# A finer split of a 512-point transform, quartered weight loads on three queues, and a priority table, in a spectral filter plus GEGLU kernel

## The chip, the cores and the metric

One core of one Trainium2 chip. The metric is device microseconds for one execution. TensorE (PE) multiplies, with its weight loads shown as PEld; VectorE (DVE), ScalarE (ACT) and GpSimd (POOL) do the rest; SyncE (SP) mostly issues DMAs, which ACT and POOL can issue too. Each engine works through its own queue in order and waits on semaphores for the others.

## The reference

The output is the sum of the input, a frequency-domain filter of its normalized rows, and a GEGLU layer of the same normalized rows:

```python
xn = _layernorm(x, axis=-1)                 # x: 1 x 2048 x 512, bf16
X  = rfft2(xn) * (w_r + 1j * w_i)           # over 2048 and 512; w: 2048 x 257
A  = irfft2(X)
h  = gelu(xn @ w_gate) * (xn @ w_up)        # 512 x 1792 each
out = x + A + h @ w_down                    # 1792 x 512
```

## The kernel before, in words

**The work.** The 2048 rows are 16 tiles of 128 rows (index j), in four blocks of four tiles (index m). For each tile DVE takes statistics (L617, L623, L631), POOL or ACT and DVE the reciprocal root (L626, L632, L633), and DVE or ACT writes the normalized row `xn` in one instruction (`ln_norm`, L641 to L647). PE transposes `xn` (`trans`, L657) and DVE or ACT copies the result to `xnT` (L668, L669): 512 features in four chunks of 128 partitions, 512 rows in the free dimension. Both branches read `xnT`.

**GEGLU.** `gate_up` (L917) makes one slice `fc` of 128 hidden features for one block: four matmuls with the gate weights (one for each chunk of features), four with the up weights (L930), a gelu on ACT (L934) and a product on DVE (L940, or L937 and L938). There are 14 slices. Block 0 does its first four slices in two halves, tiles 0 and 1 and then tiles 2 and 3, so that it can begin before the whole block is there. Blocks 2 and 3 use seven products in place of eight (`gate_up7`, L1011); the down projection does so in all blocks (L1105, and L1120 at the very end).

**Spectral branch.** The 512-point transform of a block is `butter` and `unit_D`. `butter` (L679) adds and subtracts the two halves of the features (L683, L684: 1024 elements each) and then adds and subtracts the halves of the sum (L685, L686: 512 each). `unit_D` (L688) multiplies each tile with constants `fd`: 128 columns for L697, 128 for L698, and 256 columns each for L699 and L700, which accumulate the part of the odd frequencies from the difference that was not split further. ACT writes the result to `xs` (L703). `unit_A` (L717, L720) takes the next step, its result goes through DRAM (`scr`, `tv`), and the products with the filter (L805, L826) and the way back (L855, L877) follow from about 74 us on.

**What sets the order.** Every instruction, DMAs included, is a task of a planner (`_Plan`, L215) with an engine, an estimated cost and a priority `prio`. The planner plays the tasks through in its own estimate of time: whenever an engine is free it takes, of the tasks that are ready, the one with the lowest priority number, with a bonus for a PE task of the same mode as the one before. The result is a fixed order for each engine's queue. Priorities come from a dictionary of constants, `K`, and from the arguments of the calls. A task with a `gate` also waits until the main products have come to that number.

**Loads at the start.** `load_w` (L570) loads a range of slices of one weight as one DMA: eight DMAs, all on SP, for slices 0 to 4, 4 to 8, 8 to 11 and 11 to 14 of gate and up. Tiles 0 and 1 of `x` come in halves of 64 partitions on SP and ACT, all later tiles on SP. Seventeen dummy matmuls (`warm`, L1203) run ahead of and between the first transposes.

Of the kernel before, what the change touches and what calls it, by code (L numbers as in the profile page):

```python
# [7 lines left out]
ACT = mybir.ActivationFunctionType  # L8
# [6 lines left out]
D = 512  # L15
# [14 lines left out]
def _constants():  # L30
# [9 lines left out]
    m64 = np.arange(64)[None, :]  # L40
    a0 = tp * (p + 0.5) * (4 * m64) / D
    a2 = tp * (p + 0.5) * (4 * m64 + 2) / D
    im0 = -np.sin(a0)
# [77 lines left out]
    for i, (a, b) in enumerate(((c, s), (-s, c), (-c, -s))):  # L121
# [8 lines left out]
            f16(CM), f16(G.reshape(P, -1)), f16(NA))  # L130

# [83 lines left out]
class _Plan:  # L215
# [37 lines left out]
    def schedule(self):  # L253
# [26 lines left out]
        def refill():  # L280
# [4 lines left out]
            t.i, t.eng, t.fn, t.r, t.w, t.over = len(T), "pe", (lambda e: self.fill(e, b)), (("wg", 0, 0), ("wg", 0, 1)), (("bank", b),), ()  # L285
# [136 lines left out]
def bass_parallel_sum__spectral_gfnet__glu_gated_geglu__prompt_kernel(  # L422
# [25 lines left out]
    with ExitStack() as es:  # L448
# [19 lines left out]
        tmp = area[:, 0:1024].rearrange("p (a c) -> p a c", a=2)  # L468
# [3 lines left out]
        AREA = [("tmp",)] + [("fold", i, k) for i in range(2) for k in range(3)] + [("xs", i) for i in range(4)]  # L472
# [94 lines left out]
        def wkey(nm, fs, dcs=(0, 1)):  # L567
# [13 lines left out]
        add("pool", lambda e: e.memset(nn, 0.0), w=[("nz",)], occ=1.0, lat=1.2, prio=-99)  # L581
# [22 lines left out]
        load_w("g", 11, 14, "sp", -88)  # L604
        load_w("u", 11, 14, "sp", -87)
# [35 lines left out]
        def ln_norm(j, prio, eng="dve"):  # L641
            if eng == "act":
                act(lambda e: e.activation(xn[:, j % 4, :], x_sb[:, j, :], ACT.Identity, bias=nmr[:, j:j + 1], scale=rstd[:, j:j + 1]), 770,
                    [("x", j, 0), ("x", j, 1), ("nmr", j), ("rstd", j)], [("xn", j % 4)], prio)
                return
            add("dve", lambda e: e.tensor_scalar(xn[:, j % 4, :], x_sb[:, j, :], ag[:, j, 0:1], rstd[:, j:j + 1], ALU.subtract, ALU.mult),
                r=[("x", j, 0), ("x", j, 1), ("ag", j), ("rstd", j)], w=[("xn", j % 4)], occ=0.33, lat=0.47, prio=prio)  # L647

        def trans(m, dcs, jjs, prio, eng="dve"):
# [9 lines left out]
            pe(f, [P] * (len(dcs) * len(jjs)), [("ident",)] + [("xn", jj) for jj in jjs], [("ps", v), ("tr", m, dcs, jjs)], prio, alloc=(v, 1, False))  # L659
# [19 lines left out]
        def butter(m, prio):  # L679
            f = fold[m % 2]  # L680
            k = ("fold", m % 2)
            x = xnT[m]
            dve(lambda e: e.tensor_tensor(tmp, x[:, 0:2, :], x[:, 2:4, :], ALU.add), 1024, xk(m), [("tmp",)], prio, x=2)  # L683
            dve(lambda e: e.tensor_tensor(f[:, 2:4, :], x[:, 0:2, :], x[:, 2:4, :], ALU.subtract), 1024, xk(m), [k + (1,)], prio, x=2)  # L684
            dve(lambda e: e.tensor_tensor(f[:, 0, :], tmp[:, 0], tmp[:, 1], ALU.add), 512, [("tmp",)], [k + (0,)], prio, x=2)  # L685
            dve(lambda e: e.tensor_tensor(f[:, 1, :], tmp[:, 0], tmp[:, 1], ALU.subtract), 512, [("tmp",)], [k + (2,)], prio, x=2)  # L686

        def unit_D(j, prio):  # L688
# [6 lines left out]
            def fn(e):  # L695
                o = bank(v).rearrange("p (a r c) -> p a r c", a=2, r=4)
                e.matmul(o[:, :, 0, :], f[:, 0, c], fd[:, 0:128], start=True, stop=False, skip_group_check=True)  # L697
                e.matmul(o[:, :, 2, :], f[:, 1, c], fd[:, 128:256], start=False, stop=False, skip_group_check=True)  # L698
                e.matmul(o[:, :, 1::2, :], f[:, 2, c], fd[:, 256:512], start=False, stop=False, skip_group_check=True)  # L699
                return e.matmul(o[:, :, 1::2, :], f[:, 3, c], fd[:, 512:768], start=False, stop=True, skip_group_check=True)  # L700
            pe(fn, [P, P, 256, 256], [("fd",)] + [k + (i,) for i in range(3)], [("ps", v)], prio, alloc=(v, 1, False), full=True)
# [212 lines left out]

        gun = [0]

        def gate_up(m, fc, jjs, prio, soft=()):  # L917
            k = gun[0] % 3
            gun[0] += 1
            n = len(jjs) * P  # L920
# [457 lines left out]
```

## Time and profile before

| What | Value |
|---|---|
| Runs | median 178.47 us (178.37 to 178.93, 3 runs) |
| Profiled execution | 177.96 us, of which the span is 175.80 us |
| Granted TensorE clock, mean | 0.999 |
| Busy in the span | PE 169.7, DVE 151.5, ACT 115.9, POOL 60.1 us |
| First gate product | starts at 7.46 us |
| Last matmul group | starts at 170.73 us |

The span is what the profile covers; 2.16 us of the profiled execution lie outside it. In the profile's rows, the time of an instruction runs from its start to its end; instructions of one engine overlap, since the next one starts before the last has drained. What an instruction costs its engine is therefore the distance between two starts (its pitch), which is shorter than its duration. "Idle before" names what ended a wait.

### The profile page before, as it was taken

How to read it: one execution, taken by the hardware profiler on the slowest of the kernel's cores; microseconds unless marked ns; L12 is line 12 of the kernel's file. 1: busy time of each engine (PE TensorE's matmuls, PEld its weight loads, DVE VectorE, ACT ScalarE, POOL GpSimd, SP SyncE). 2: the span in 40 equal slices, each digit the busy share in tenths (PEclk: the TensorE clock that was granted, in tenths of full speed). 3: DMA queues.
4: the chain of work that ended last, by engine and by line, in shares of the span. 5: the costliest groups of instructions: out<-in, count | busy, mean ns of one | idle time of the engine just before them, and what ended most of it. 6: DMA issues, size and time to landing. Idle time of an engine off the chain costs nothing.

```text
span 175.8 us, 4162 instructions
## 1 busy us (share of the span) xinstructions
PE 169.7 (97%) x1580; PEld 124.0 (71%) x1580; DVE 151.5 (86%) x346; ACT 115.9 (66%) x193; POOL 60.1 (34%) x104
## 2 busy tenths in 40 slices
PE   7989999999999999999999999999999999999992
PEld 2557555557758854444787788887889998888881
DVE  2689799979798755699699899998999999999992
ACT  3625997779973223388853899889928699996200
POOL 2020205458816368888678100004145120000000
PEclk9999999999999999999999999999999999999999
DMA  3999996898867877575898942400022223100013
GB/s 77 308 319 309 267 266 182 242 296 223 192 134 111 165 202 194 146 228 151 205 258 234 237 124 60 123 0 0 6 60 56 69 60 84 39 0 4 0 30 90
DMA packets 20819, 25.26 MB, mean 144 GB/s; under 512 B 3232, under 2 KB 16928, under 8 KB 20544
## 3 DMA queue, kind: packets, MB, share of 16 engines
q1 hardware_dynamic: 17088, 17.21, 36.4%
q0 software_dynamic: 3120, 7.47, 18.2%
q10 hardware_dynamic: 592, 0.33, 0.7%
q8 instruction: 12, 0.20, 0.5%
q14 instruction: 7, 0.06, 0.1%
HBM read 18.70 MB, written 6.29 MB: 142 GB/s over the span
## 4 chain that ended last, share of the span: by engine, by line
PE 83%; DVE 9%; DMA 3%; SPq 2%; issue 1%; DVEq 0%
PE ps L930 25%; PE ps L1105 23%; PE ps L1011 20%; DMA x_sb<-in_A_x_dram 3%; PE ps L826 3%; PE ps L877 2%; PE ps L657 2%; PE ps L855 2%; SPq L560 2%; PE ps L805 1%; DVE hT L1038 1%; DVE hT L1042 1%; PE ps L699 1%; PE ps L700 1%; PE ps L717 1%
## 5 line engine op out<-in xcount | busy, mean ns | idle before, releaser
L930 PE MATMUL ps<-xw,wu 128*128 128x512 f16 (+1 forms) x128 | 29.3, 353 | 0.5 <-DMA wu<-in_B_w_up_dram 0.5
L930 PE MATMUL ps<-xw,wg 128*128 128x512 f16 (+1 forms) x128 | 29.0, 353 | 0.2 <-DVE xw L668 0.2
L934 ACT ACTIVATE gl<-ps 128x512 bf16<-128x512 f32 (+1 forms) x32 | 17.3, 546 | 17.7 <-PE ps L930 17.6
L862 POOL COPY bc<-tv 1x128 bf16<-1x128 bf16 x16 | 8.7, 558 | 39.6 <-ACT bc L861 39.6
L940 DVE TENSOR_TENSOR hT<-ps,gl 128x512 bf16<-128x512 f32 (+1 forms) x26 | 15.4, 602 | 6.5 <-PE ps L930 5.6
L930 PEld LDWEIGHTS ps<-xw,wu 128*128 128x128 bf16 x128 | 12.0, 98 | 11.3 <-DMA wu<-in_B_w_up_dram 0.7
L930 PEld LDWEIGHTS ps<-xw,wg 128*128 128x128 bf16 x128 | 11.9, 98 | 10.6 <-DMA wg<-in_B_w_gate_dram 0.6
L613 POOL DMA_DIRECT2D xw<-in_A_w_r_dram x28 | 16.2, 612 | 7.9 <-PE ps L930 5.0
L1024 ACT ACTIVATE gl<-ps 128x512 bf16<-128x512 f32 x28 | 17.1, 632 | 2.1 <-PE ps L1011 1.2
L613 POOL DMA_DIRECT2D xw<-in_A_w_i_dram x28 | 16.1, 601 | 3.7 <-PE ps L1105 2.5
L1011 PE MATMUL ps<-xn,ws 128*128 128x256 f16 x112 | 16.2, 273 | 0.0
L1011 PE MATMUL ps<-xn,wu 128*128 128x256 f16 x112 | 16.0, 273 | 0.0
L1011 PE MATMUL ps<-xw,wg 128*128 128x256 f16 x112 | 16.0, 273 | 0.0
L1105 PE MATMUL ps<-wd,hT 128*128 128x256 bf16 x112 | 13.6, 273 | 0.0
L617 DVE BATCH_NORM_STATS2 st<-x_sb 128x6 f32<-128x512 bf16 x16 | 10.5, 683 | 3.5 <-DMA x_sb<-in_A_x_dram 3.3
L1105 PE MATMUL ps<-wd,hs 128*128 128x256 f16 (+1 forms) x112 | 13.4, 273 | 0.0
L1105 PE MATMUL ps<-wdt,hs 128*128 128x256 f16 x112 | 13.1, 273 | 0.0
L626 POOL TENSOR_TENSOR rstd<-vpe,mhalf 128x4 f32<-128x4 f32 (+1 forms) x5 | 4.6, 923 | 23.0 <-DVE vpe L624 23.0
L1105 PEld LDWEIGHTS ps<-wd,hT 128*128 128x128 bf16 x112 | 10.6, 98 | 2.1 <-ACT bc L861 0.3
L1105 PEld LDWEIGHTS ps<-wdt,hs 128*128 128x128 f16 x112 | 10.8, 98 | 1.6 <-issue 0.2
L1105 PEld LDWEIGHTS ps<-wd,hs 128*128 128x128 f16 x112 | 10.8, 98 | 1.6 <-DVE mu L1140 0.2
L1011 PEld LDWEIGHTS ps<-xw,wg 128*128 128x128 bf16 x112 | 10.7, 98 | 1.6 <-issue 0.2
(132 smaller groups left out, 381.9 us busy)
## 6 DMA issues: line engine op xcount, KB each, us to landing
scr<-ta SPq DMA_DIRECT2D x32, 64.0 KB, 4.9
tv<-scr SPq DMA_DIRECT2D x8, 256.0 KB, 5.6
scr<-bc SPq DMA_DIRECT2D x16, 128.0 KB, 3.1
area<-scr SPq DMA_DIRECT2D x8, 256.0 KB, 4.2
xw<-in_A_w_r_dram POOLq DMA_DIRECT2D x28, 64.0 KB, 3.8
xw<-in_A_w_i_dram POOLq DMA_DIRECT2D x28, 64.0 KB, 3.6
x_sb<-in_A_x_dram SPq DMA_DIRECT2D x6, 256.0 KB, 10.4
out_dram<-x_sb SPq DMA_DIRECT2D x12, 128.0 KB, 2.3
```

The source lines that it names most:

```text
L560: return add(eng, lambda e: e.dma_start(dst, src), r=r, w=w, over=over, occ=occ, lat=kb / 1024 / rate, prio=prio, dma=True)
L613: add("pool", lambda e: e.dma_start(dst, src), r=r, w=w, over=over, occ=0.7, lat=kb / 1024 / 0.27, prio=prio, gate=prio, dma=True)
L617: add("dve", lambda e: e.bn_stats(st[:, j, :], x_sb[:, j, :]), r=[("x", j, 0), ("x", j, 1)] + behind, w=[("st", j)], occ=0.6, lat=0.75, pr ...
L626: add("pool", lambda e: e.tensor_tensor(rstd[:, sl], vpe[:, sl], mhalf[:, 0:n], ALU.pow), r=[("vpe", j) for j in js] + [("mhalf",)], w=[(" ...
L826: ins = e.matmul(bank(v, hh)[64 * kl:64 * kl + 64, 256 * z:256 * z + 256], cm[64 * hh:64 * hh + 64, 2 * H + z, kl, i, :], pp[i][64 * hh:64 ...
L862: add("pool", lambda e: e.tensor_copy(z[0:1, 1, :].rearrange("o (b q) -> o b q", b=2), z256[0:1, :].rearrange("o (b j q) -> o b j q", b=2, ...
L930: ins = e.matmul(bank(v)[:, 0:n], w_sb[nm][:, dc, fc * P:(fc + 1) * P], xnT[m][:, dc, c0:c0 + n], start=(dc == 0), stop=(dc == 3))
L934: act(lambda e: e.activation(gl[k][:, 0:n], bank(vs[0])[:, 0:n], ACT.Gelu_apprx_tanh), n, [("ps", v)], [("gl", k)], prio)
L940: dve(lambda e: e.tensor_tensor(o, bank(vs[1])[:, 0:n], gl[k][:, 0:n], ALU.mult), n, [("ps", vs[1]), ("gl", k)], ks, prio + K["dH"])
L1011: ins = e.matmul(bank(v)[:, 256 * q:256 * q + 256], W_, B0[:, dc, :], start=(first and q == 0 and dc == 0), stop=(dc == 1), skip_group_che ...
L1024: act(lambda e: e.activation(gl[k][:], bank(v), ACT.Gelu_apprx_tanh), 512, [("ps", v)], [("gl", k)], prio + K["aG"])
L1105: ins = e.matmul(bank(v)[:, 256 * t:256 * t + 256], A0[:, f, P * t:P * t + P], B0[:, f, :], start=(first and t == 0 and f == 0), stop=(f = ...
```

## The change

It has five parts.

1. **The 512-point transform is split once more.** `ln_norm` now writes the features of a row in another order, in two instructions: in chunks 0 and 2 the two groups of 64 change places, in chunks 1 and 3 each group of 64 is reversed. With it `butter` splits the difference as well as the sum (four instructions of 512 elements in place of two), and `unit_D` becomes four matmuls of 128 columns each. `fd` shrinks from 768 to 512 columns. `tmp` becomes two buffers. The constants follow the new order.
2. **Weights.** Since the features have a new order, the rows of the gate and up weights are loaded in it: four DMAs for each range (two halves of 64 partitions for chunks 0 and 2, and one each for chunks 1 and 3). The ranges become 0 to 2, 2 to 4, 4 to 9 and 9 to 14, so 32 DMAs in place of 8. For slices 0 to 4, chunks 1 and 3 are issued by POOL; one DMA of the up weights goes to ACT, and so does one half of tiles 2 and 3 of `x`.
3. **First gate products.** For slices 0 and 1 of block 0 the gate product of two tiles is made tile by tile (128 columns at a time, eight matmuls in place of four).
4. The two dummy matmuls behind the second transpose go.
5. **Order.** A table `ORDER` gives the priority of every one of the 1072 tasks, and `GATES` the gates; they replace what `K` and the arguments set. The bonus for the same PE mode becomes 1.0 (it was 12.67).

The diff, cut to its core; the other hunks rename keys or adapt constants to the new order.

```diff
+    r = np.arange(P)[:, None] ^ 64
+    ae, ao = tp * (r + 0.5) * 2 * m / D, tp * (r + 0.5) * (2 * m + 1) / D
+    im0 = -np.sin(ae)
     im0[:, 0] = (-1.0) ** np.arange(P)
-    fo = []
-    for c in range(2):
-        kodd = np.concatenate([4 * m64[0] + 1, 4 * m64[0] + 3])[None, :]
-        a = tp * (p + P * c + 0.5) * kodd / D
-        fo += [np.cos(a), -np.sin(a)]
-    FD = np.concatenate([np.cos(a0), im0, np.cos(a2), -np.sin(a2)] + fo, 1)
+    FD = np.concatenate([np.cos(ae), im0, np.cos(ao), -np.sin(ao)], 1)
...
+ORDER = [
+    -578, 187, -235, -1622, -2527, -3409, -3271, -3914, -3516, -3004, -2669, -3101, -2614, -2693, -2697, -167, -2069, -1900, -2211, -842, -1854, -1431, -725, -541,
...
+]
+GATES = {281: 6146, 282: 5379, 283: 4832, 300: 2591, 301: 3138,
...
-        tmp = area[:, 0:1024].rearrange("p (a c) -> p a c", a=2)
+        tmp = [area[:, 1024 * i:1024 * i + 1024].rearrange("p (a c) -> p a c", a=2) for i in range(2)]
...
-        def load_w(nm, lo, hi, eng, prio, dcs=(0, 1)):
-
-            src = (B_w_gate if nm == "g" else B_w_up).rearrange("(dc p) f -> p dc f", p=P)
+        def load_w(nm, lo, hi, eng, prio, odd=None, second=None):
+
+
+            src = (B_w_gate if nm == "g" else B_w_up).rearrange("(dc i p) f -> i p dc f", i=2, p=P)
             cs = slice(P * lo, P * hi)
-            ds = slice(2 * dcs[0], 2 * dcs[-1] + 2)
-            dma(eng, w_sb[nm][:, ds, cs], src[:, ds, cs], w=wkey(nm, range(lo, hi), dcs), prio=prio, kb=64 * len(dcs) * (hi - lo))
+            n = hi - lo
+            for a in range(2):
+                dma((eng, second or eng)[a], w_sb[nm][64 * a:64 * a + 64, ::2, cs], src[0][64 - 64 * a:128 - 64 * a, :, cs], w=[(k, f, a) for k, f, _ in wkey(nm, range(lo, hi), (0,))],
+                    prio=prio + 0.01 * a + (4 if second and a else 0), kb=32 * n)
+            for i in range(2):
+                v = src[1][:, i, cs].rearrange("(a q) f -> a q f", a=2)[:, ::-1]
+                dma(odd or eng, w_sb[nm][:, 2 * i + 1, cs], v, w=[(k, f, 2 + i) for k, f, _ in wkey(nm, range(lo, hi), (0,))], prio=prio + 0.02 + 0.01 * i, kb=32 * n)
...
         dma("sp", ident[:], c_id.ap(), w=[("ident",)], prio=-99.2, kb=32)
-        load_w("g", 0, 4, "sp", -99)
+        load_w("g", 0, 2, "sp", -99, "pool")
         load_x(2, 2, 0, "sp", -98.5)
-        load_x(2, 2, 1, "sp", -98)
-        load_w("u", 0, 4, "sp", -97)
-        load_w("g", 4, 8, "sp", -96)
-        load_w("u", 4, 8, "sp", -95)
+        load_x(2, 2, 1, "act", -98)
+        load_w("u", 0, 2, "sp", -97.5, "pool")
+        load_w("g", 2, 4, "sp", -97, "pool")
+        load_w("u", 2, 4, "sp", -96.5, "pool", "act")
+        load_w("g", 4, 9, "sp", -96)
+        load_w("u", 4, 9, "sp", -95)
         amv = c_am.ap().rearrange("p (j r c) -> p j r c", j=NJ, r=2)
 
         def load_am(m, prio, eng="sp"):
             dma(eng, am[:, 4 * m:4 * m + 4], amv[:, 4 * m:4 * m + 4], w=[("am", m)], prio=prio, kb=256)
         load_x(4, 4, 0, "sp", -94.5)
         load_x(4, 4, 1, "sp", -94)
-        dma("sp", fd[:], c_fd.ap(), w=[("fd",)], prio=-93, kb=192)
+        dma("sp", fd[:, 0:512], c_fd.ap(), w=[("fd",)], prio=-93, kb=128)
         load_am(0, -92.5)
-        load_w("g", 8, 11, "sp", -92)
-        load_w("u", 8, 11, "sp", -91)
+        load_w("g", 9, 14, "sp", -92)
+        load_w("u", 9, 14, "sp", -91)
...
         def ln_norm(j, prio, eng="dve"):
-            if eng == "act":
-                act(lambda e: e.activation(xn[:, j % 4, :], x_sb[:, j, :], ACT.Identity, bias=nmr[:, j:j + 1], scale=rstd[:, j:j + 1]), 770,
-                    [("x", j, 0), ("x", j, 1), ("nmr", j), ("rstd", j)], [("xn", j % 4)], prio)
-                return
-            add("dve", lambda e: e.tensor_scalar(xn[:, j % 4, :], x_sb[:, j, :], ag[:, j, 0:1], rstd[:, j:j + 1], ALU.subtract, ALU.mult),
-                r=[("x", j, 0), ("x", j, 1), ("ag", j), ("rstd", j)], w=[("xn", j % 4)], occ=0.33, lat=0.47, prio=prio)
+
+            xq = x_sb[:, j, :].rearrange("p (d i a c) -> p i d a c", i=2, a=2, c=64)
+            o = xn[:, j % 4, :].rearrange("p (d i a c) -> p i d a c", i=2, a=2, c=64)
+            for i, (xi, oi) in enumerate(((xq[:, 0], o[:, 0][:, :, ::-1]), (xq[:, 1], o[:, 1][:, :, :, ::-1]))):
+                if eng == "act":
+                    act(lambda e, xi=xi, oi=oi: e.activation(oi, xi, ACT.Identity, bias=nmr[:, j:j + 1], scale=rstd[:, j:j + 1]), 500,
+                        [("x", j, 0), ("x", j, 1), ("nmr", j), ("rstd", j)], [("xn", j % 4, i)], prio)
+                else:
+                    add("dve", lambda e, xi=xi, oi=oi: e.tensor_scalar(oi, xi, ag[:, j, 0:1], rstd[:, j:j + 1], ALU.subtract, ALU.mult),
+                        r=[("x", j, 0), ("x", j, 1), ("ag", j), ("rstd", j)], w=[("xn", j % 4, i)], occ=0.2, lat=0.33, prio=prio)
...
-            dve(lambda e: e.tensor_tensor(tmp, x[:, 0:2, :], x[:, 2:4, :], ALU.add), 1024, xk(m), [("tmp",)], prio, x=2)
-            dve(lambda e: e.tensor_tensor(f[:, 2:4, :], x[:, 0:2, :], x[:, 2:4, :], ALU.subtract), 1024, xk(m), [k + (1,)], prio, x=2)
-            dve(lambda e: e.tensor_tensor(f[:, 0, :], tmp[:, 0], tmp[:, 1], ALU.add), 512, [("tmp",)], [k + (0,)], prio, x=2)
-            dve(lambda e: e.tensor_tensor(f[:, 1, :], tmp[:, 0], tmp[:, 1], ALU.subtract), 512, [("tmp",)], [k + (2,)], prio, x=2)
+            t, d = tmp[0], tmp[1]
+            dve(lambda e: e.tensor_tensor(t, x[:, 0:2, :], x[:, 2:4, :], ALU.add), 1024, xk(m), [("tmp", 0)], prio, x=2)
+            dve(lambda e: e.tensor_tensor(d, x[:, 0:2, :], x[:, 2:4, :], ALU.subtract), 1024, xk(m), [("tmp", 1)], prio, x=2)
+            for i, (s, op) in enumerate(((t, ALU.add), (t, ALU.subtract), (d, ALU.subtract), (d, ALU.add))):
+                dve(lambda e, i=i, s=s, op=op: e.tensor_tensor(f[:, i, :], s[:, 0], s[:, 1], op), 512, [("tmp", i // 2)], [k + (i,)], prio, x=2)
...
-                o = bank(v).rearrange("p (a r c) -> p a r c", a=2, r=4)
-                e.matmul(o[:, :, 0, :], f[:, 0, c], fd[:, 0:128], start=True, stop=False, skip_group_check=True)
-                e.matmul(o[:, :, 2, :], f[:, 1, c], fd[:, 128:256], start=False, stop=False, skip_group_check=True)
-                e.matmul(o[:, :, 1::2, :], f[:, 2, c], fd[:, 256:512], start=False, stop=False, skip_group_check=True)
-                return e.matmul(o[:, :, 1::2, :], f[:, 3, c], fd[:, 512:768], start=False, stop=True, skip_group_check=True)
-            pe(fn, [P, P, 256, 256], [("fd",)] + [k + (i,) for i in range(3)], [("ps", v)], prio, alloc=(v, 1, False), full=True)
+                ins = None
+                for i in range(4):
+                    ins = e.matmul(bank(v)[:, P * i:P * i + P], f[:, i, c], fd[:, P * i:P * i + P], start=(i == 0), stop=(i == 3), skip_group_check=True)
+                return ins
+            pe(fn, [P] * 4, [("fd",)] + [k + (i,) for i in range(4)], [("ps", v)], prio, alloc=(v, 1, False), full=True)
...
+                np_ = parts if nm == "g" else 1
+                w = n // np_
+                for i in range(np_):
+                    def fn(e, nm=nm, v=v, i=i, w=w):
+                        ins = None
+                        for dc in range(4):
+                            ins = e.matmul(bank(v)[:, w * i:w * i + w], w_sb[nm][:, dc, fc * P:(fc + 1) * P], xnT[m][:, dc, c0 + w * i:c0 + w * i + w],
+                                           start=(dc == 0 and i == 0), stop=(dc == 3), skip_group_check=True)
+                        return ins
+                    js = jjs[len(jjs) // np_ * i:len(jjs) // np_ * (i + 1)]
+                    kw = dict(alloc=(v, 1, False)) if i == 0 else {}
+                    pe(fn, [w] * 4, wkey(nm, [fc]) + xk(m, js) + [("d1", m - 1)], [("ps", v)], prio + (0.0 if nm == "g" else 0.0017 * n) + (0.05 * i if np_ > 1 else 0.0), full=(n == 512), main=True, **kw)
...
-        warm(2, -42.9, [("tr", 0, (0, 1, 2, 3), (1,))])
...
-                    gate_up(0, fc, (0, 1), gu_at[(0, fc, 0)])
-                    gate_up(0, fc, (2, 3), gu_at[(0, fc)])
+                    gate_up(0, fc, (0, 1), gu_at[(0, fc, 0)], 2 if fc < 2 else 1)
+                    gate_up(0, fc, (2, 3), gu_at[(0, fc)], 2 if fc < 2 else 1)
...
+        for t, v in zip(pl.tasks, ORDER):
+            t.prio = v / 100
+            t.gate = GATES[t.i] / 100 if t.i in GATES else None
+        pl.bonus = 1.0
```

More of the change, by code (lines that the diff above doesn't have):

```diff
@@ L471, in bass_parallel_sum__spectral_gfnet__glu_gated_geglu__prompt_kernel @@
         vv = area[:].bitcast(BF16).rearrange("p (l c) -> p l c", l=32)
-        AREA = [("tmp",)] + [("fold", i, k) for i in range(2) for k in range(3)] + [("xs", i) for i in range(4)]
+        AREA = [("tmp", 0), ("tmp", 1)] + [("fold", i, k) for i in range(2) for k in range(4)] + [("xs", i) for i in range(4)]
         ta = sb("ta", [P, 2048], F16)
@@ L658, in f @@
                 return ins
-            pe(f, [P] * (len(dcs) * len(jjs)), [("ident",)] + [("xn", jj) for jj in jjs], [("ps", v), ("tr", m, dcs, jjs)], prio, alloc=(v, 1, False))
+            pe(f, [P] * (len(dcs) * len(jjs)), [("ident",)] + [("xn", jj, i) for jj in jjs for i in range(2)], [("ps", v), ("tr", m, dcs, jjs)], prio, alloc=(v, 1, False))
             w = len(jjs) * P
```

36 lines of the change are left out of this document (13 added, 23 removed), and 51 rows, old and new, of tables (GATES, ORDER).

## The prediction, before the changed kernel was run

> **What bounds the kernel now.** I read the page's head first: who is busy for how long. Then the chain of waits, then the busy time by stages, then the start instruction by instruction.
>
> ```profile
> span 175.8 us, 4162 instructions
> ...
> PE 169.7 (97%) x1580; PEld 124.0 (71%) x1580; DVE 151.5 (86%) x346; ACT 115.9 (66%) x193; POOL 60.1 (34%) x104
> ...
> PE 83%; DVE 9%; DMA 3%; SPq 2%; issue 1%; DVEq 0%
> ```
>
> PE carries 83% of the chain that ended last. The stages show where it isn't full, and who comes next. Columns: stage, its length, then the busy time of PE, PEld, DVE, ACT, POOL (instructions in brackets), granted clock, DMA share, GB/s.
>
> ```profile
> 0.00:12.84 12.84, 10.56 (x65) 5.63 (x66) 7.39 (x23) 5.30 (x10) 2.32 (x8) 1.00 0.81 235
> 12.84:52.00 39.16, 39.10 (x318) 24.61 (x319) 35.57 (x94) 31.82 (x54) 16.41 (x24) 1.00 0.90 237
> 52.00:74.00 22.00, 22.00 (x150) 13.49 (x148) 14.65 (x27) 7.51 (x12) 13.96 (x23) 1.00 0.72 160
> ...
> 101.00:171.00 70.00, 69.59 (x715) 60.90 (x714) 68.40 (x153) 53.07 (x95) 8.74 (x16) 1.00 0.18 45
> ```
>
> From 12.84 us on PE is full: work taken from PE shortens the run if nothing else becomes late. DVE is close behind: 3.59 us idle from 12.84 to 52, 7.35 from 52 to 74, 1.60 from 101 to 171. The start, from the timeline of PE (start, duration, idle before and its releaser at the end):
>
> ```profile
> 6.69 0.59 PE L1203 MATMUL ps<-hs 128*128 128x512 f16 x2
> 7.46 1.91 PE L930 MATMUL ps<-xw,wg 128*128 128x256 f16 x16 [0.18 <-DVE xw L668]
> 9.84 0.61 PE L930 MATMUL ps<-xw,wu 128*128 128x256 f16 x4 [0.47 <-DMA wu<-in_B_w_up_dram]
> 10.82 0.40 PE L657 MATMUL ps<-ident,xn 128*128 128x128 f16 x4 [0.37 <-DVE vpe L624]
> 11.05 1.04 PE L930 MATMUL ps<-xw,wu 128*128 128x256 f16 x8
> 11.97 0.40 PE L657 MATMUL ps<-ident,xn 128*128 128x128 f16 x4
> ```
>
> Useful work begins at 7.46: the gate weights (issued at 2.64) and the copies of tile 1 (L668, 6.89 to 7.31) are both only then there. Between 7.46 and 12.84 PE does 32 matmuls of 256 columns (0.109 us pitch) and two transposes (0.22 each): 3.9 of 5.4 us, so some 1.45 us are holes, for the up weights (landed 9.8) and for tiles 2 and 3, whose second half lands at 8.34, 4.67 us after its issue behind the weights.
>
> **The transform's PE work.** One `unit_D`, from the timeline:
>
> ```profile
> 42.95 0.22 PE L697 MATMUL ps<-fd,area 128*128 128x128 f16 x1
> 43.01 0.22 PE L698 MATMUL ps<-fd,area 128*128 128x128 f16 x1
> 43.06 0.27 PE L699 MATMUL ps<-fd,area 128*128 128x256 f16 x1
> 43.17 0.27 PE L700 MATMUL ps<-fd,area 128*128 128x256 f16 x1
> 43.28 0.22 PE L697 MATMUL ps<-fd,area 128*128 128x128 f16 x1
> ```
>
> Start to start a unit takes 0.33 us: two matmuls of 128 columns at 0.055 and two of 256 at 0.11. Four of 128 take 0.22; the transposes (16 in 0.89 us in the chain) confirm 0.055 with a weight load for each. 16 units save 16 x 0.11 = **1.77 us**, all between 17 and 52 us, where PE is full. ACT's copy (L703, 0.61 us, same 512 elements) is unchanged.
>
> **Its price on DVE.** `butter` at 40 us starts L683 at 40.01, L684 at 40.60, L685 at 41.21, L686 at 41.54, and the next instruction at 41.88: pitch 0.60 for 1024 elements, 0.335 for 512. Two more of 512 add 0.67 a block, **2.7 us** in four. `ln_norm` in one piece has pitch 0.335 (three L646 from 21.90, 1.05 us in all); by the line through 1024 and 512 elements, a half has 0.20, so a tile costs 0.40: 0.07 more, 0.8 us for 12 tiles on DVE. No normalization here writes backwards; L887 and L890 do in another operation, and take 0.414 and 0.415 us where their forward neighbours L886 and L889 take 0.415 and 0.416. I take no penalty; were the reversed half at half speed (256 elements at 0.26 us instead of 0.13), 1.6 us more. On ACT the four tiles that L643 does (0.81 each) become eight halves: nothing more by L669's 0.38 for 256 elements, 3.2 us more if each half took the 0.81 of the whole. I take the former; ACT has 7.3 us idle in that stage, which hides either.
>
> So DVE gets some 3.3 us more work before 52 us (four butterflies and eight norms), where PE's work shrinks by 1.77: 35.57 + 3.3 = 38.9 in 37.4 us. **It does not fit** unless DVE work moves behind 52 us. It can: the sums for block 2 (L982 to L985, 1.4 us at 45 to 47), not used before 96 us, and the sums of the down weights (1.5 us there). That is 2.9, and 52 to 74 has 7.35 us idle. Full cover is too much to ask, since 3.59 us of idle are waits for others; I charge PE **0.5 us**, between 0 and 3.3.
>
> **The weights.** Four DMAs in place of each one, same bytes: for slices 0 to 4, 1 MB with tiles 0 to 3 and `ident` 1.57 MB. SP's issues go from 24 to 38 before `scr` begins, at pitch 0.55 to 0.6: 38 x 0.58 = 22 us, against 19.2 now (with pauses inside the rows up to 2.72 us) and the first `scr` issue at 22.05. Cost at the end: nothing, as `tv` is read only at 74. But what is late in SP's queue lands late: by the table `am` for the first `unit_A` is about SP's 26th to 27th issue (some 16 us, where it is 7.87 now) and one part of the up weights of slices 4 to 9 the 25th (14.7). PE has work until about 18 us without them (block 0's first four slices, gate products, `unit_D`), so I take no wait, between 0 and 2 us. POOL issues eight DMAs of 64 KB, about 0.6 us each (L613's median 0.59), where it only filled `nn` and then idled to 9.60. ACT issues two more (0.65 each), before and after its table load by the table, which can move the first square root from 4.36 to 4.85; the first tile's normalization then just precedes the second's, and tile 1 is not later than now.
>
> Tile 0's copy ends at 6.68 now. If slices 0 and 1 of the gate weights are there (SP's seventh issue, 3.7 us, plus 2.5 us as for 64 KB of `x`; POOL's third, 2.3 plus 3.8 as for 64 KB of L613), the first gate product starts at 6.9 in place of 7.46: 0.5 us. Eight matmuls of 128 columns cost what four of 256 do (8 x 0.055 = 4 x 0.11). Tiles 2 and 3 can land near 7.3 in place of 8.34, so that of the 1.45 us of holes about half may close. I take **1.0 us** for the start (0 to 1.95, and below zero by the 2 us above). The dummy pair that goes (0.43 us) stood where PE waited anyway.
>
> [...] Weights, `x` and tables move at 338 GB/s from 5 to 12 us (busy time by stages). [...]
>
> **The table.** After 12.84 PE's holes are few: 0.53 us at 119, 0.2 each at 50 and 123, and 0.1 us at each change of tile shape (as 34.78 to 34.88). A new order could gain at most about 1.5 us and could lose as much; I take 0. The tail, from the last matmul's end (172.3) to 175.8, is DVE's addition and the output DMAs (2.2 us to landing) and stays.
>
> **Sum**, against the profiled execution: 177.96 - 1.77 - 1.0 + 0.5 = 175.7. The runs' median is 0.5 above that execution (178.47), so the forecast is **175.9 us** with a little less than all of that difference.
>
> **Rivals.**
> (a) *Weights come no sooner.* The engines' throughput sets the landing, the start gains nothing, the transform's saving stays: 178.5 - 1.77 + 0.3 = 177.0 (176.4 to 177.9). For it: DMA share at or above 0.9 from 5 us on. Against: the dip from 3 to 5 us. [...]
> (b) *DVE becomes the bound up to 52 us* and the run is **slower**. Its place: `butter` of blocks 2 and 3 (40 to 50 us), where the chain already runs through DVE from 45.04 to 50.26. If nothing moves behind 52 us and the 3.59 us of waits stay, the stage takes 38.9 + 3.6 = 42.5 for 39.16, and with the start's gain the run is 178.5 + 3.3 - 1.0 = 180.8. It decides as soon as DVE's lateness exceeds what is saved, 2.8 us. Against it: 2.9 us of movable work.
> (c) *All eaten*: DVE or late loads cost about 2.5 us, and the time stays near 178.4.
> (d) *More than forecast*: the holes at the start close and the table takes half of the later ones: 178.5 - 1.77 - 1.9 - 0.6 = 174.2.
>
> **Chances**: forecast (174.7 to 176.4) 0.44, (a) 0.20, (b) 0.14, (c) 0.07, (d) 0.15. Faster by over 0.3% (0.53 us, about what a measurement of this kernel can tell from no change) is forecast, (a) and (d): 0.79; same 0.07; slower 0.14. The range takes in (d), the forecast, (a) and (c), 0.86 less the edges: 173.6 to 178.6.
>
> **What the profile will show.** Right: `unit_D` at pitch 0.22; first gate product before 7.1 us; holes before 12 us under 0.9 us; DVE near full from 13 to 50 us with the sums for block 2 later. Wrong: PE waits for `area` or `xw` written by DVE between 20 and 50 us (b), PE waiting for `wu`, `wg` or `ac` before 20 us (a, c), or a reversed half of `ln_norm` well over 0.3 us.

## The result, and the profile after

| | before | after |
|---|---|---|
| Runs beside each other | median 178.50 us (178.37 to 178.93, 4 runs) | median 210.75 us (209.78 to 211.90, 4 runs) |
| Profiled execution | 177.96 us | 210.02 us |
| Span | 175.8 us | 208.2 us |

The ratio is 1.180 [1.175, 1.185] (here and below to runs of the kernel before on the same chip, with a 95% interval): 32 us slower, where 175.9 us was forecast. In what follows, line numbers are those of each kernel: the gate and up products are L930 before, L996 after; the DMA issues L560 and L613.

The page of the kernel after: span, busy times, granted clock in 40 slices of 5.2 us (in tenths of full speed), DMA rate in the same slices, and the chain (shares of the span by what carried it; SPq is SyncE's queue of DMA issues).

```profile
span 208.2 us, 4249 instructions
...
PE 178.0 (85%) x1594; PEld 125.6 (60%) x1594; DVE 155.7 (75%) x366; ACT 118.6 (57%) x197; POOL 67.1 (32%) x112
...
PEclk9979757878569999999999999999999999999999
...
GB/s 102 151 137 74 157 47 165 131 116 147 213 163 228 199 142 187 125 164 182 224 107 157 204 216 230 203 151 104 2 3 35 20 50 101 54 50 3 0 25 77
...
PE 46%; SPq 20%; DVE 15%; DMA 7%; ACT 5%; POOL 3%; issue 3%; DVEq 0%; ACTq 0%
```

The rate before, in 40 slices of 4.4 us:

```profile
GB/s 77 308 319 309 267 266 182 242 296 223 192 134 111 165 202 194 146 228 151 205 258 234 237 124 60 123 0 0 6 60 56 69 60 84 39 0 4 0 30 90
```

PE's share of the chain fell from 83% to 46%, and SP's queue, 2% before, holds 20%. In the first eight slices 47 to 165 GB/s move, where before it was 77 and then 182 to 319. The stages of the prediction again (same columns):

```profile
12.84:52.00 39.16, 20.54 (x145) 11.76 (x143) 18.40 (x58) 13.80 (x27) 3.44 (x5) 0.81 0.48 121
52.00:74.00 22.00, 19.09 (x127) 10.22 (x128) 12.57 (x34) 10.54 (x17) 10.06 (x15) 0.80 0.76 197
74.00:101.00 27.00, 26.35 (x219) 16.62 (x216) 23.07 (x53) 17.05 (x26) 16.79 (x26) 1.00 0.72 170
101.00:171.00 70.00, 69.70 (x753) 52.78 (x752) 63.95 (x139) 52.65 (x84) 28.13 (x52) 1.00 0.46 119
```

From 12.84 to 52 us PE is busy for 20.5 of 39.2 us, at a clock of 0.81, and the DMA engines are half idle. From 74 us on PE is nearly full again (the same stretches of time hold earlier work than before, since the kernel is some 32 us behind). So nearly all is lost in the first 74 us. Over the whole span PE is idle for 30.2 us, where it was 6.1, and busy for 8.3 us more: together the 32 us. PE's waits (total us, times, longest):

```profile
PE ps L996 <- DMA wg<-in_B_w_gate_dram: 14.5, 3, 8.7
PE ps L996 <- DMA wu<-in_B_w_up_dram: 6.7, 2, 4.4
PE ps L720 <- DMA ident<-c_id: 3.1, 1, 3.1
```

24.3 us in six waits, for three tensors. SP's timeline (start, duration, issues) shows why they are late:

```profile
9.52 1.36 SPq L613 DMA_DIRECT2D x_sb<-in_A_x_dram  x1
10.92 5.67 SPq L613 DMA_DIRECT2D wg<-in_B_w_gate_dram  x2
16.63 0.53 SPq L613 DMA_DIRECT2D wu<-in_B_w_up_dram  x1
17.20 4.49 SPq L613 DMA_DIRECT2D wg<-in_B_w_gate_dram  x1
21.73 0.61 SPq L613 DMA_DIRECT2D wu<-in_B_w_up_dram  x1
...
43.91 0.54 SPq L613 DMA_DIRECT2D wu<-in_B_w_up_dram  x1
```

An issue takes some 0.6 us. Seven in this stretch take 3.3 to 5.1 (the row of 5.67 holds one of 0.56 and one of 5.06). The last of the weights are issued at 43.9 us, and land at 58.0. And while SP stands, little flows; columns as above:

```profile
26.00:32.00 6.00, 2.13 (x7) 0.90 (x8) 0.46 (x1) 0.20 (x1) 0.00 (x0) 0.50 0.14 47
```

A DMA share of 0.14 is 2.2 of 16 engines, at 47 GB/s. In this stretch PE comes out of its longest hole (8.69 us, ended at 29.87) with a granted clock of 0.50. By the clock records of the trace the granted clock stood at 0.50 in four stretches of the first 61 us, and PE was busy for 15.9 us in them. There a matmul of 512 columns starts 0.427 us after the one before and one of 128 columns 0.107, where at 1.00 it is 0.216 and 0.056. At the full clock that work would take half the time, by this estimate 8 us less. So much PE's busy time grew by, although its work shrank.

### The profile page after: what moved, and what is told of

Same layout as the page of the kernel before. It is cut to its first block, busy times and chain, and to the rows that moved or that the text cites. A ratio compares the mean times of both kernels' runs of the same rounds, so it can differ in the third digit from the quotient of the medians.

```text
span 208.2 us, 4249 instructions
## 1 busy us (share of the span) xinstructions
PE 178.0 (85%) x1594; PEld 125.6 (60%) x1594; DVE 155.7 (75%) x366; ACT 118.6 (57%) x197; POOL 67.1 (32%) x112
## 4 chain that ended last, share of the span: by engine, by line
PE 46%; SPq 20%; DVE 15%; DMA 7%; ACT 5%; POOL 3%; issue 3%; DVEq 0%; ACTq 0%
SPq L613 20%; PE ps L1174 15%; PE ps L996 12%; PE ps L1080 11%; DMA wu<-in_B_w_up_dram 7%; DVE hT L1107 2%; PE ps L889 2%; POOL bc L925 1%; DVE area L750 1%; POOL rstd L685 1%; PE ps L940 1%; PE ps L720 1%; DVE hT L1111 1%; ACT gl L1093 1%; ACT bc L924 1%
## 5 line engine op out<-in xcount | busy, mean ns | idle before, releaser
L996 PE MATMUL ps<-xw,wg 128*128 128x512 f16 (+2 forms) x144 | 32.1, 367 | 14.6 <-DMA wg<-in_B_w_gate_dram 14.5
L1003 ACT ACTIVATE gl<-ps 128x512 bf16<-128x512 f32 (+1 forms) x32 | 17.2, 550 | 33.8 <-PE ps L996 30.2
L996 PE MATMUL ps<-xw,wu 128*128 128x512 f16 (+1 forms) x128 | 30.1, 377 | 6.7 <-DMA wu<-in_B_w_up_dram 6.7
L996 PEld LDWEIGHTS ps<-xw,wg 128*128 128x128 bf16 x144 | 13.7, 108 | 26.8 <-issue 9.7
L996 PEld LDWEIGHTS ps<-xw,wu 128*128 128x128 bf16 x128 | 12.2, 103 | 19.5 <-issue 11.0
L925 POOL COPY bc<-tv 1x128 bf16<-1x128 bf16 x16 | 8.0, 519 | 48.7 <-ACT bc L924 48.4
L672 POOL DMA_DIRECT2D xw<-in_A_w_r_dram x28 | 17.2, 640 | 16.1 <-PE ps L996 14.5
L676 DVE BATCH_NORM_STATS2 st<-x_sb 128x6 f32<-128x512 bf16 x16 | 10.7, 684 | 14.8 <-DMA x_sb<-in_A_x_dram 14.6
L672 POOL DMA_DIRECT2D xw<-in_A_w_i_dram x28 | 17.5, 625 | 13.1 <-PE ps L996 8.4
L685 POOL TENSOR_TENSOR rstd<-vpe,mhalf 128x4 f32<-128x4 f32 (+1 forms) x5 | 5.7, 1143 | 28.1 <-DVE vpe L683 28.1
L1174 PE MATMUL ps<-wd,hs 128*128 128x256 bf16 (+1 forms) x112 | 13.6, 273 | 0.1
L731 DVE COPY xw<-ps 128x512 f16<-128x512 f16 (+2 forms) x5 | 2.5, 503 | 14.6 <-PE ps L720 14.6
L1174 PEld LDWEIGHTS ps<-wdt,hs 128*128 128x128 f16 x112 | 10.7, 98 | 2.2 <-DVE wdt L1143 0.8
```

The costliest lines, as they stand in the source:

```text
L672: add("pool", lambda e: e.dma_start(dst, src), r=r, w=w, over=over, occ=0.7, lat=kb / 1024 / 0.27, prio=prio, gate=prio, dma=True)
L676: add("dve", lambda e: e.bn_stats(st[:, j, :], x_sb[:, j, :]), r=[("x", j, 0), ("x", j, 1)] + behind, w=[("st", j)], occ=0.6, lat=0.75, pr ...
L685: add("pool", lambda e: e.tensor_tensor(rstd[:, sl], vpe[:, sl], mhalf[:, 0:n], ALU.pow), r=[("vpe", j) for j in js] + [("mhalf",)], w=[(" ...
L925: add("pool", lambda e: e.tensor_copy(z[0:1, 1, :].rearrange("o (b q) -> o b q", b=2), z256[0:1, :].rearrange("o (b j q) -> o b j q", b=2, ...
L996: ins = e.matmul(bank(v)[:, w * i:w * i + w], w_sb[nm][:, dc, fc * P:(fc + 1) * P], xnT[m][:, dc, c0 + w * i:c0 + w * i + w], start=(dc == ...
L1003: act(lambda e: e.activation(gl[k][:, 0:n], bank(vs[0])[:, 0:n], ACT.Gelu_apprx_tanh), n, [("ps", v)], [("gl", k)], prio)
```

## Experiments

**First series: which part of the loads.** The DMAs of chunks 1 and 3 are the only ones whose rows are read as two groups of 64, each backwards. Theory: their row pattern makes them slow. Rivals: the backwards step alone, SP's queue alone, the table.

`e1_forward`, on the changed kernel; rows in plain order, so that the GEGLU products meet rows in a wrong order (this holds for all kernels below whose weights are in plain order or in groups):

```diff
-                v = src[1][:, i, cs].rearrange("(a q) f -> a q f", a=2)[:, ::-1]
+                v = src[1][:, i, cs]
```

> The changed kernel with one edit: the weight DMAs of chunks 1 and 3 take their 128 rows in order and not reversed in two groups of 64 (the GEGLU branch then gets rows in a wrong order, the work is the same). Theory A (these DMAs, written as two groups of 64 rows, run on 2 of the 16 DMA engines and hold up SP's queue, about 27 us, while the start itself costs some 5 us for other reasons): SP's issues of 3 to 5 us vanish, holes of 4 to 9 us on PE after 20 us vanish, time 180 to 184 us, first gate product still after 9 us. Theory B (everything comes from these DMAs): 175 to 178 us, first gate product near 7 us. Theory C (the table's order of SP's queue is what makes the weights late): above 195 us.

Measured: 182.35 us, 1.017 [1.008, 1.026]. 28 of the 32 us are this one line. SP's stalls are gone, and of PE's waits for DMA 3.5 us are left:

```profile
PE ps L996 <- DMA wg<-in_B_w_gate_dram: 1.9, 3, 1.1
...
PE ps L762 <- DMA fd<-c_fd: 1.0, 1, 1.0
PE ps L720 <- DMA ident<-c_id: 0.6, 1, 0.6
```

`e2_two_groups`: two groups of 64 rows again, forward, 256 rows apart, so that they don't join into one run: `v = src[1][64 * i:64 * i + 64, :, cs].rearrange("q d f -> d q f")`.

> The changed kernel with the same DMAs in two groups of 64 rows, but forward rows that lie 256 rows apart, so that they can't be joined to one run of 128 (rows in a wrong order for the GEGLU branch). Theory A (two groups as the outermost step put the DMA on 2 engines): 205 to 213 us as the changed kernel, with stretches at some 40 packets of 1280 bytes per us. Rival (reading backwards is what is slow): 176 to 184 us.

Measured: 212.81 us (one run), as the change. The stretch of 26 to 32 us looks the same as well:

```profile
26.00:32.00 6.00, 1.48 (x4) 0.57 (x5) 0.00 (x0) 0.00 (x0) 0.00 (x0) 0.50 0.16 49
```

Reading backwards is innocent; the two groups are not.

`e3_all_pool`: the DMAs as changed, but those of chunks 1 and 3 all on POOL (`dma("pool", ...)` in place of `dma(odd or eng, ...)`).

> The changed kernel with all DMAs of chunks 1 and 3 issued by POOL, still reversed in two groups (the eight of slices 4 to 14 move from SP to POOL). Theory A, if POOL's DMAs spread over all engines as the eight at the start seem to: no stretch on 2 engines, SP's issues of 3 to 5 us vanish, 179 to 186 us. If POOL's are on 2 engines as well, the time stays at 200 us or more. Rival (reversed rows are slow on any queue): above 200 us.

Measured: 223.46 us, 1.247 [1.236, 1.258]. My expectation missed: taking the DMAs off SP ends SP's stalls of 3 to 5 us (the longest issue is 2.7 us), and the time gets longer, so SP's queue is not the cause but where it shows. The rival's window (above 200 us: slow on any queue) held, for two groups and not for the backwards step. On POOL the same pattern is slow in another way. The pages give the packet counts of after, of `e1_forward` and of `e3_all_pool`:

```profile
DMA packets 21092, 25.24 MB, mean 121 GB/s; under 512 B 4400, under 2 KB 17072, under 8 KB 20816
```
```profile
DMA packets 20308, 25.21 MB, mean 140 GB/s; under 512 B 3616, under 2 KB 16288, under 8 KB 20032
```
```profile
DMA packets 22227, 25.26 MB, mean 114 GB/s; under 512 B 6304, under 2 KB 17952, under 8 KB 21952
```

Under 512 B there are 784 packets more than in `e1_forward` in the change, and 2688 more in `e3_all_pool`. The packet records show what is new on POOL's queue: 896 packets of 32 B in both, and 1792 of 16 B in `e3_all_pool`, seven for each packet of 4 or 5 KB; why they are there stays open. In the changed kernel a 64 KB piece of `wg` from POOL lands 7.5 us after its issue (median); in `f5_full_partitions` below, with plain rows, 3.2.

`e4_forward_no_table`: `e1_forward` without `ORDER` and `GATES`.

> As the run with rows in order, and without the table: priorities and gates from the constants and arguments (GEGLU rows in a wrong order). It tells what the table is worth once the DMAs are spread. If the table's SP order (ident and tile 2 behind weights) makes the late start: 176 to 180 us, at least 2 us under the run with rows in order. If the table is good and the start is bound by the small pieces: as that run or up to 5 us above it.

Measured: 185.64 us, 1.033 [1.023, 1.044]. The table is no cause of the loss; with these loads it is worth some 3 us over the constants (runs of 184.2 to 186.3 us against 181.3 to 183.2).

**Second series: how many groups.** If the outermost step of a DMA sets how many of the 16 engines it runs on, four groups must give four and 16 groups all of them. On `e1_forward`; `src4` is the same weight seen as `(a q) f` with a groups, each DMA taking 128 / a rows of each. `k16_groups`, with a = 16 (`k4_groups` has a = 4 and 32 rows in place of 8):

```diff
-                v = src[1][:, i, cs]
+                v = src4[:, 8 * i:8 * i + 8, cs]
```

> e1_forward with the DMAs of chunks 1 and 3 reading four groups of 32 rows, 128 rows apart, in place of 128 rows in a row (the rows are not the right ones; bytes, sizes and queues are the same). Theory (a DMA from SP goes to as many of the 16 DMA engines as its outermost step has groups): stretches in which about 4 engines are busy, some 75 packets of 1280 B per us in place of 38, SP's stalls about half as long, time between e1 and e2: 186 to 200. Rival (any row order that doesn't join into one run is slow alike): 210 as with two groups.

> The same with 16 groups of 8 rows, 32 rows apart. Theory (outermost groups set the number of engines): no stretch with few engines, SP's issues at 0.6 us, time as e1_forward, 181 to 184. Rival (unjoined rows): 200 to 212.

Measured: 194.98 us, 1.092 [1.085, 1.099], and 182.01 us, 1.019 [1.013, 1.026]. Both as the theory had it. Two stretches of `k4_groups` in which SP stands for part of the time, and two of about the same place in `k16_groups`:

```profile
18.00:22.00 4.00, 1.11 (x11) 0.71 (x8) 2.64 (x8) 1.04 (x4) 0.00 (x0) 1.00 0.34 106
28.00:29.50 1.50, 1.50 (x11) 0.61 (x8) 0.33 (x1) 1.50 (x4) 0.00 (x0) 1.00 0.39 75
```
```profile
18.00:22.00 4.00, 2.74 (x26) 1.59 (x24) 3.40 (x8) 2.51 (x5) 0.00 (x0) 1.00 1.09 255
26.00:32.00 6.00, 4.86 (x22) 1.91 (x21) 5.17 (x16) 4.58 (x8) 2.45 (x4) 1.00 1.05 231
```

DMA share 0.14, 0.34 to 0.39, 1.05 to 1.09: some 2, 6 (by the theory 4, and a little of other transfers) and all 16 engines; 47, 75 to 106, 231 to 255 GB/s. (The share adds up the times of packets, so it can pass 1.) SP issues eight such pieces of 160 KB, 1.31 MB in all: at 47 GB/s that is 28 us, by this estimate the loss between `e1_forward` and the change. So for 2, 4 and 16 groups the number of busy engines went with the number of groups; other counts were not run.

The trace after names no engine, but its landings fit the same two each time. A DMA spread over all engines lands in 16 parts. Of `fd`, issued at 23.03 us, fourteen parts land between 26.14 and 26.82, and two at 30.95 and 31.66. Every other spread DMA that SP issues between 11.5 and 44.5 us has two such stragglers, the first of them 4.0 to 6.4 us behind the rest, the second 4.8 to 7.0. The last two parts of the two-group pieces land one piece behind the other (28.84 and 29.41, 34.98 and 36.29, 38.57 and 39.47 us). In `k4_groups` four parts of 16 straggle in the same way, by 4.2 to 7.2 us for DMAs issued from 10.7 to 34 us; in `e1_forward` the last two are at most 0.7 us behind. By these landings the eight pieces queue up on the same two engines, and a DMA spread over all 16 is complete only when its share there has come through behind them. That is how `x`, `am` and `fd` became late, too.

**Third series: the rest, 182 to 178.** With plain rows the change still wasn't faster than before, though PE's work is 1.8 us shorter.

`f5_full_partitions`: `e1_forward`, and chunks 0 and 2 also in DMAs over all 128 partitions, one chunk each, same number, size and queue (`src` here has the chunk first):

```diff
-                dma((eng, second or eng)[a], w_sb[nm][64 * a:64 * a + 64, ::2, cs], src[0][64 - 64 * a:128 - 64 * a, :, cs],
+                dma((eng, second or eng)[a], w_sb[nm][:, 2 * a, cs], src[2 * a, :, cs],
```

> e1_forward with the DMAs of chunks 0 and 2 each over all 128 partitions as well (one chunk per DMA, same number, size and queue; products of gate and up meet rows in the wrong order). Theory (pieces over 64 partitions move slower): the rate from 9 to 16 us rises from 219 to about 290 GB/s, and the time falls by 1.5 to 3 us to 179 to 181. Rival (the rate is held by the number of small DMAs or by POOL and the queues, not by their partitions): unchanged, 182 to 183, rate 210 to 230.

Measured: 179.32 us, 1.001 [0.997, 1.005]. DMA rate from 9 to 16 us in `e1_forward`, then here:

```profile
9.00:16.00 7.00, 6.96 (x76) 5.68 (x73) 6.18 (x20) 3.06 (x8) 1.18 (x2) 1.00 0.97 219
```
```profile
9.00:16.00 7.00, 6.74 (x70) 5.36 (x68) 6.18 (x21) 2.79 (x8) 1.19 (x2) 1.00 0.98 258
```

At the same share, 258 GB/s in place of 219 (I had said 290): pieces over 64 partitions move slower, which cost some 1.6% more. Sizes and numbers of packets are the same in both traces. `k16_groups`, measured on the chip of `f5_full_partitions` and with the same halves as `e1_forward`, has 1.019, so the chip is not what differs. Why the halves move slower is not shown.

`f1_transform_only`: the changed transform with the loads of before, no table:

```diff
+            dma(eng, w_sb[nm][:, :, cs], src[:, :, cs], w=wkey(nm, range(lo, hi)), prio=prio, kb=128 * (hi - lo))
```

> The changed transform alone: unit_D in four matmuls of 128 columns, butter with two more differences, the normalization in halves. The weights are loaded as before, one DMA per slice range on SP with rows in their order (so the products of gate and up meet rows in the wrong order; times only), no table, gate products in one piece. Theory (the loss is all in the loads, the transform gives its 1.8 us on PE less what DVE adds): 0.5 to 1.8 us under before, 176.7 to 178 against 178.5, and the DMA rate from 9 to 16 us is back near 307 GB/s. Rival (the transform's price on DVE is larger than its saving, so that it costs by itself): 179 or more, with PE waits for area or xw between 13 and 52 us.

Measured: 179.12 us, 1.001 [0.997, 1.005], above the theory's window and in the rival's. The transform alone, in an order planned anew for it, brings nothing either.

`f6_one_dma_table` (one DMA per range and the table without the dropped entries) and `f3_ident_fd_early` (two of the 1072 entries changed: `{9: -33.5, 38: -10.0}`):

> e1_forward with one DMA per weight and slice range, all on SP, in row order, and the table with the entries of the dropped DMAs left out: what the split in four on three queues costs, apart from the order of rows. Theory (what is left of e1's loss is the split): 177 to 180, rate from 9 to 16 us near 300. Rival (what is left is the table's order, which puts ident, fd and tile 2 late): 181 to 183.

> e1_forward with two entries of the table changed: ident and fd are issued earlier on SP. Theory (these two are only late because the weights before them are slow; each cost PE about 0.6 to 1.0 us): 180.5 to 181.5. Rival (the bytes ahead are what is late, and something else takes their place): 182 to 183.

Measured: 199.94 us, 1.116 [1.107, 1.125], and 197.93 us, 1.105 [1.098, 1.113]. Both missed and tell nothing of what they were made for: PE is idle for 22.7 and 20.4 us in all, where `e1_forward` has 10.0. From 100 to 175 us alone it is 8.2 and 7.5 us against 0.4, with the longest hole (3.0 us) behind ACT's write of `bc`, far from the edit. The planner plays the table through, and another order at the start gives another order everywhere.

`h1_dve_as_before` and `h2_norm_whole`, which are `f1_transform_only` with `xn` written by one instruction again, and the first also with the difference written straight to `f[:, 2:4, :]`, fell into the same trap:

> f1_transform_only with DVE's work as before: the normalization in one piece and butter in four operations (the last two differences of the second half are left out, so the transform's odd outputs are not right); unit_D stays at four matmuls of 128 columns. Theory (the 1.8 us that unit_D saves on PE are eaten by DVE's added work): 176.5 to 177.3, about 1.8 under before. Rival (saved PE time turns into waits whatever DVE does, as for x or psum banks): 178.2 to 179.2, as f1.

> f1_transform_only with the normalization in one piece alone (features not permuted, so the transform is not right), butter in six operations. Theory (halving the normalization and the two more differences share the price, 0.8 and 2.7 us of DVE): 177.5 to 178.6. Rival (the halved normalization is the whole price, since it stands ahead of the first products): 176.7 to 177.2.

Measured: 189.02 us, 1.060 [1.054, 1.065], and 185.84 us, 1.041 [1.035, 1.047]: *less* work, 7 to 10 us more than `f1_transform_only`, with several holes of 0.5 to 1.1 us on PE after 125 us. A change of a task's cost re-plans the run.

**Fourth series: prices with the order held fixed.** These edit the kernel before inside the tasks and leave the planner's costs alone, so that every engine's order stays as it was. `b1_narrow_d` takes the saving (first two pairs of lines), `b2_more_dve` the price (a second operation in the same task, and the normalization in two halves), `b3_both` both:

```diff
-                e.matmul(o[:, :, 1::2, :], f[:, 2, c], fd[:, 256:512], start=False, stop=False, skip_group_check=True)
-                return e.matmul(o[:, :, 1::2, :], f[:, 3, c], fd[:, 512:768], start=False, stop=True, skip_group_check=True)
+                e.matmul(o[:, :, 1, :], f[:, 2, c], fd[:, 256:384], start=False, stop=False, skip_group_check=True)
+                return e.matmul(o[:, :, 3, :], f[:, 3, c], fd[:, 512:640], start=False, stop=True, skip_group_check=True)
...
+                e.tensor_tensor(area[:, 1024 + 512 * (nd[0] % 2):1536 + 512 * (nd[0] % 2)], tmp[:, 0], tmp[:, 1], op)
                 return e.tensor_tensor(o, tmp[:, 0], tmp[:, 1], op)
```

> The kernel before, with its order of work untouched, and the last two matmuls of unit_D narrowed from 256 to 128 columns (they write one half each and leave out the other, so the odd outputs are not right). Theory (PE work taken out where PE is full shortens the run): 1.77 us under before, 176.7. Rival (the saved time turns into waits even with DVE as it was): 178 to 178.8.

> The kernel before, order untouched, with the change's work added on DVE and ACT alone: two more 512-element operations in each butter (their results go to an unused place) and each normalization in two halves. Theory (about 3.3 us of DVE work before 52 us that do not fit beside PE): 1 to 3 us over before, 179.5 to 181.5. Rival (DVE's idle time there takes it in): 178.4 to 179.0.

> Both edits together, order untouched: the price of the transform's change in the kernel before, without loads and table. Theory (the saving is eaten by DVE, as f1 suggests): 178 to 179.5, the sum of the other two. Rival (the two add up to less, since the narrowed unit_D gives DVE's results more slack): 176.7 to 177.8.

Measured: 178.95 us, 1.003 [1.000, 1.006]; 182.46 us, 1.021 [1.018, 1.025]; 183.80 us, 1.026 [1.021, 1.031]. PE's 1.77 us give nothing, about the rival's result. The added work of `b2_more_dve` costs 3.8 us (0.0214 x 178.4), above the theory's window. It is more than the 3.3 us that the theory named; busy times of `b2_more_dve`:

```profile
PE 171.9 (95%) x1580; PEld 123.7 (69%) x1580; DVE 156.4 (87%) x366; ACT 116.9 (65%) x197; POOL 62.5 (35%) x104
```

DVE has 4.9 us more than before, and ACT 1.0. `b3_both` missed both windows, though the theory's sentence held: it costs about the sum of the other two (4.6 against 0.6 and 3.8 us). In its profiled execution the granted clock also fell to 0.50 for 3.4 us. The chain of `b1_narrow_d`, and its PE waits after 30 us:

```profile
PE 64%; DVE 20%; ACT 4%; DMA 3%; issue 3%; POOL 2%; SPq 2%; ACTq 0%; DVEq 0%
```
```profile
PE ps L930 <- DVE hT L940: 0.6, 1, 0.6
PE ps L1105 <- DVE mu L1140: 0.5, 1, 0.5
```

Before, the chain was 83% PE and 9% DVE; with PE a little shorter it runs mostly through DVE from 12.8 to 38 us, and PE waits for results that had been just in time. From the 61st to the 481st matmul, the same work but for the narrowed ones, the trace before takes 50.98 us and `b1_narrow_d` 51.91; behind that both take 109.02 (one execution each).

`b4_less_dve` lets `butter` fold only the first tile of each block (`[:, 0:P]` on every operand), which `unit_D` then uses for all four (`c = slice(0, P)`; the other tiles' transform is left out); `b5_less_both` narrows `unit_D` as well.

> The kernel before, order untouched, with DVE's butter cut to a quarter: it folds the first tile of each block only, and unit_D uses that tile for all four (the transform of the other tiles is left out). DVE does some 4.8 us less before 52 us, PE the same. Theory (from 13 to 52 us PE and DVE are both full, so that taking from one of them gives nothing): 178.0 to 178.6, no more than 0.4 us under before. Rival (DVE alone sets the pace, and PE only looks full): 174 to 177.

> b4_less_dve with unit_D narrowed to four matmuls of 128 columns as in b1_narrow_d: work taken from both. Theory (both are bounds): PE's 1.77 us now come through, 176.2 to 177.0, where b1_narrow_d alone gave nothing. Rival (a third thing, DMA or ACT, holds the time): 178 to 178.8.

Measured: 177.94 us, 0.997 [0.994, 1.000], and 177.99 us, 0.998 [0.995, 1.000]. DVE does 4.3 us less up to 52 us and the time is 0.5 us lower, with an interval that just reaches 1.000; the theory had at most 0.4. Both less: no better, against the theory. A third thing is in the chain of `b5_less_both` from 39 us on (start, duration):

```profile
39.17 1.02 ACT xw L669
40.20 0.49 ACT gl L934
...
41.27 1.51 ACT xn L643 x2
42.79 0.49 ACT ps L1154
...
43.29 0.60 ACT gl L934
43.89 1.43 ACT area L703 x3
...
45.69 1.08 ACT xw L669
```

ACT works almost without a pause (7.81 of 8.00 us from 39 to 47; 7.98 before), and the chain runs behind it. From 50.69 to 57.25 it then runs through DVE's preparation of the down weights (L1073 to L1140). From the 61st to the 481st matmul `b5_less_both` takes 50.94 us against 50.98 before, with some 1.75 us less work. The largest delays that are new are 0.66 us at 56.5 behind DVE (L1140) and 0.2 us at 46.5 behind ACT; the others are under 0.2 us each, and their releasers were not all followed up. So the saving on PE is used up in several small waits: ACT and DVE were that close behind.

## Why the prediction was wrong, step by step

- **Weights: the step that failed.** "Four DMAs in place of each one, same bytes", and from it "no wait, between 0 and 2 us". I priced the DMAs by issues and bytes. But in two groups of rows they ran on some two of the 16 engines (DMA share 0.14), in 16 groups on all of them (1.05 to 1.09). Measured, 24.3 us of PE's waits, where 0 to 2 were allowed, and a granted clock of 0.50 behind them; 28.4 us between the change and `e1_forward`. The halves of 64 partitions, also "same bytes", cost some 3 us more (182.35 against 179.32). POOL's issues, priced at 0.6 us each, took 0.80 to 0.97.
- **unit_D: size right, worth nothing.** In the trace after the four matmuls start 0.055 to 0.056 us apart, so a unit takes the 0.22 us that were forecast, and the saving is there. But "work taken from PE shortens the run" had the condition "if nothing else becomes late", and that condition failed at once (`b1_narrow_d`, `b5_less_both`).
- **DVE.** `butter`'s pitches are as worked out, and the reversed half has no penalty (the plain halves of `b2_more_dve` have the same pitch, 0.25 us). A half of `ln_norm` has that pitch, not 0.20: 2.0 us in 12 tiles, where 0.8 was taken. So the added work is some 4.7 us by the pitches (DVE is busy for 4.9 us more in `b2_more_dve`). I charged 0.5 us, since sums could move behind 52 us; in the old order the added work costs 3.8 (`b2_more_dve`, in which ACT has 1.0 us more as well). Re-planned, saving and price come out even: 179.1 and 179.3. Rival (b), DVE as the bound, named a mechanism that is there in the old order; it does not set the time of a re-planned kernel, and it is not what made the change slow.
- **Start.** The first gate product came at 11.42 us, not 6.9; with plain, full-width rows (`f5_full_partitions`) at 7.72, against 7.46 before. So three queues and halved ranges bring no earlier start even then: rival (a). The dip before 5 us that spoke against (a) (156 GB/s from 2.6 to 5 us in the kernel before, 338 from 5 to 12) did not become one. The holes behind it do shrink: the first up product starts at 8.74, where it was 9.84, and by 13.05 us matmuls worth 36 of 256 columns are done, against 32 by 12.84 before. That is an estimated 0.2 us (4 x 0.109 less 0.21), where 1.0 was taken.
- **Table.** Taken at 0. It is worth some 3 us over the constants on its own task list (`e4_forward_no_table`). With two entries changed or 24 tasks left out, the time is 16 to 18 us longer (`f3_ident_fd_early`, `f6_one_dma_table`).
- **The sum.** 175.7 and the 0.5 us by which the median lies above the profiled execution make 176.2; 175.9 takes only 0.2 of that difference. The 1.57 MB are the weights with the four tiles, without `ident`. Neither decided anything.

Of the 32 us: 28 from the two-group pattern, 3 from halves of 64 partitions, 0 to 1 from all the rest, where 1.8 us less work on PE brings no gain. No version here beats the kernel before by more than the measurement tells: the two that come out lower, `b4_less_dve` and `b5_less_both`, leave out part of the transform. A correct load in the new row order that spreads over all engines was not tried.

## What to carry to other kernels

Read a DMA's access pattern from the outside in before pricing it by bytes: in these runs the outermost count (2, 4, 16) went with the number of engines it ran on (DMA share 0.14, 0.34 to 0.39, 1.05 to 1.09), and halves of 64 partitions moved slower than all 128 (219 against 258 GB/s). Where PE is full, ask for each of its inputs how early it was there; here other engines were as close to late, and 1.77 us taken from PE bought nothing (178.95 us in `b1_narrow_d`, against 178.36). To price a part of a planned kernel, keep the plan fixed, or the new order is what you measure. And a PE that is shown busy all the time can still hide waits: an instruction's time reaches into the next one's (a matmul of 128 columns is shown for 0.22 us, and the next starts 0.055 us after it).

## Not expected

- Two groups from POOL keep all engines busy (DMA share 0.98 from 16 to 50 us in `e3_all_pool`) and yet move only 155 GB/s, where `e1_forward` moves 239 at 0.97.
- The DMAs on two engines held up their issuer: SP stood for 3.3 to 5.1 us on seven issues that take some 0.6 else, six of them of DMAs that are not in two groups themselves, and other data (`x`, `am`, `fd`) came late with them.
- The granted clock went to 0.50 in each of four holes of PE (3.1 to 8.7 us), for 3.4 to 10.2 us at a time. With the same work, PE is busy for 178.0 us where `e1_forward`, whose granted clock stays at 1.00 up to its last 3 us, has 170.6.
